# Two pairs in place of a group of four, second products at half the rate among pairs, x by DMA from tile 8 on, and a shorter lead for late tiles, in a fused retention and MLP kernel

## The chip, the cores and the metric

The kernel runs on one core of one Trainium2 chip. The metric is device time in microseconds (us), the median of several executions. The **span** is what the trace covers, from the first to the last instruction of the program; the time of an execution is some 1.8 to 2.1 us longer than its span. The engines are PE (matmuls), PEld (PE's weight loads, which overlap matmuls), DVE (VectorE), ACT (ScalarE), POOL (GpSimd) and SP (SyncE, which here only issues DMAs).

## The reference, cut to what matters

Retention over 768 steps with a decaying state, then one MLP block with a layer norm and a residual:

```python
for t in range(S):
    state = gamma[None, :, None, None] * state + np.einsum('bhd,bhe->bhde', k[:, :, t], v[:, :, t])
    y[:, :, t] = scale * np.einsum('bhd,bhde->bhe', q[:, :, t], state)
...
x = np.ascontiguousarray(attn_out.transpose(0, 2, 1, 3)).reshape(B, S, H * D)
xn = (x - mu) / np.sqrt(var + 1e-06) * g_ln
ch = np.maximum(xn @ w_ch1, 0.0) @ w_ch2
return x + ch
```

Batch 4, 8 heads, 64 values a head: 3072 rows of 512, and an MLP of 512 to 2048 to 512.

## The kernel before

The 3072 rows are 24 **tiles** of 128. For each tile the attention part makes, in this order, the scores `pa` (PE), masked scores `asb` (DVE), the output `py` (PE), its statistics and the normalised `xn` (DVE). Between chunks of a sequence, `pd` (PE) and `state` (DVE) carry the state; `vg` is v scaled on POOL for it. `trq` is q, transposed (from tile 8 on by a DMA from SP, into `tr`) and then scaled on DVE. Then x must stand transposed (`xnt`) for the **first product** (`mm`, 512 to 2048, in 16 blocks called `ho`), a ReLU on ACT, and the **second product** (`tp`, back to 512).

First products are made for groups of tiles, so that a matmul has 128, 256 or 512 columns:

```python
GROUPS = [1] * 6 + [2] * 3 + [4] * 3
...
T0, TX = 8, 11
```

x is transposed on PE for tiles below `TX`, by four matmuls against the identity and a copy by ACT. For tiles 8 to `TX` - 1 they write into the one buffer of the attention output, `py`, for earlier ones into a buffer of the second product, `tp`. From `TX` on x is transposed by a DMA from SP:

```python
if t < TX:
    xp = "tp" if t < T0 else "py"
    def e_tx(eng, t=t, xp=xp):
        p = take(xp, ("x", t), [P, KO, P], BF16)
        for ko in range(KO):
            nc.tensor.transpose(p[:, ko, :], held["xn", t][:, ko * P:(ko + 1) * P], idn)
    ...
else:
    def e_ex(eng, t=t, xb=xb, xi=xi):
        ...
        nc.sync.dma_start_transpose(out=held["xnt", xb][:, xi], in_=held["xn", t])
```

The order on every engine is made while the program is built. A small planner inside the kernel simulates the engines with assumed durations and picks, of the tasks that can start first, the one of lowest rank. Ranks come from a line of PE units, in which second products of earlier tiles (`behind`) are mixed among first products, and the attention of a tile comes 48 units ahead of its first product:

```python
for g in range(NG):
    for ho in range(HO):
        unit["1", g, ho] = u
        u += GROUPS[g] / 4
        if g >= 6 and ho % 4 == 3 and behind:
            unit["2", behind.pop(0)] = u
            u += 4
    behind += range(G0[g], G0[g] + GROUPS[g])
...
rank_of[t] = 10 * t if t < 4 else max(10 * t, 500 + unit["1", g, 0] - 48 + 8 * i)
```

So a changed rank moves instructions on all engines, and the engines then run what stands in their queues in that fixed order. The semaphores, not the planner, decide when.

Of the kernel before, what the change touches and what calls it, by code (L numbers as in the profile page):

```python
# [112 lines left out]
def kernel(  # L113
# [25 lines left out]
    HO = DH // P  # L139
    NPAIR = H // 2  # L140
    TILES = [(b, 0) for b in range(B)] + [(b, c) for b in range(B) for c in range(1, C)]
    number = {bc: t for t, bc in enumerate(TILES)}
    GROUPS = [1] * 6 + [2] * 3 + [4] * 3
    NG = len(GROUPS)
    G0 = [sum(GROUPS[:g]) for g in range(NG)]
    GMAX = max(GROUPS)
    T0, TX = 8, 11

    buf_of = {g: divmod(G0[g], GMAX) for g in range(NG)}
    group_of = {G0[g] + i: (g, i) for g in range(NG) for i in range(GROUPS[g])}  # L150

# [212 lines left out]
    unit, u, behind = {}, 0, []  # L364
    for g in range(NG):
        for ho in range(HO):
            unit["1", g, ho] = u
            u += GROUPS[g] / 4
            if g >= 6 and ho % 4 == 3 and behind:
                unit["2", behind.pop(0)] = u  # L370
                u += 4
        behind += range(G0[g], G0[g] + GROUPS[g])
    for t in behind:
# [3 lines left out]
    rank_of = {}  # L377
    for t in range(NT):
        g, i = group_of[t]
        rank_of[t] = 10 * t if t < 4 else max(10 * t, 500 + unit["1", g, 0] - 48 + 8 * i)  # L380


    ex, pbt, vgs, pbs = {}, {}, [], []
# [1 line left out]
    for t in range(NT):  # L385
        b, c = TILES[t]
        r = rank_of[t]
        g, i4 = group_of[t]
# [216 lines left out]
    for t, cols in [(t, slice(0, DM)) for t in range(NT - 1)] + [  # L605
            (NT - 1, slice(0, DM - P)), (NT - 1, slice(DM - P, DM))]:
        g, i4 = group_of[t]
# [70 lines left out]
```

## Time and profile before

| | before |
|---|---|
| time, first median of 3 | 217.09 us (216.86 to 217.13) |
| PE busy | 206.9 us, 96% of the profile's span |
| DVE, ACT, POOL busy | 56%, 40%, 42% |
| scaling of q from DMA'd tiles (`trq<-tr`), 16 times | 591 ns on average |

The profile is of another execution, of 217.65 us, 0.6 us over the median; its span is 215.8 us. What carries the reading stands in the prediction. Beside it, three groups of PE, with the counts that the change will move (busy us, mean ns | idle before):

```profile
L581 PE MATMUL mm<-xnt,w 128*128 128x512 bf16 x192 | 45.9, 379 | 0.0
...
L581 PE MATMUL mm<-xnt,w 128*128 128x256 bf16 x192 | 23.6, 273 | 0.0
...
L534 PE MATMUL py<-idn,xn 128*128 128x128 bf16 x12 | 1.2, 219 | 0.0
```

The mean of one matmul (379 ns) is not its price: matmuls overlap, and the price is the distance from one start to the next, 216 ns for 512 columns. One more group of the page, on DVE:

```profile
L425 DVE TENSOR_TENSOR trq<-tr,qsc 128x512 bf16<-128x512 bf16 x16 | 9.5, 591 | 0.3
```

### The profile page before, as it was taken

What the parts mean: (1) busy time and instruction counts of PE and PEld (TensorE: products, weight loads), DVE (VectorE), ACT (ScalarE), POOL (GpSimd) and SP (SyncE); (2) the same over time, 40 slices, a digit from 0 to 9 for tenths busy, and PEclk for the clock granted to TensorE, in tenths of its full rate; (3) what the DMA queues carried; (4) which work ended last, traced back from release to release, by engine and by line L of the source; (5) the groups of instructions that cost most, each with busy time, mean ns of one, the idle gap of its engine ahead of it and who ended that gap; (6) DMA issues with size and microseconds to landing.
All of it is one profiled execution on the core that took longest, in us unless ns stands there. A gap on an engine that the chain in (4) does not pass through costs nothing.

```text
span 215.8 us, 4578 instructions
## 1 busy us (share of the span) xinstructions
PE 206.9 (96%) x1892; PEld 130.7 (61%) x1910; DVE 120.3 (56%) x229; ACT 86.2 (40%) x158; POOL 89.7 (42%) x105
## 2 busy tenths in 40 slices
PE   7888899999999999999999999999999999999993
PEld 6777899996665567566757544554544444444442
DVE  6677577993029987999899955861511101111121
ACT  5466557774223235333316543563442334332000
POOL 8997699959953169863497100000000000000000
PEclk9999999999999999999999999999999999999999
DMA  7999999999999999999999993111121011110212
GB/s 140 179 180 181 178 155 196 206 163 150 165 162 206 153 203 146 164 143 183 184 153 177 110 225 98 49 24 29 47 73 49 3 49 49 49 49 0 100 49 97
DMA packets 106694, 26.51 MB, mean 123 GB/s; under 512 B 99377, under 2 KB 103729, under 8 KB 106674
## 3 DMA queue, kind: packets, MB, share of 16 engines
q0 software_dynamic: 75984, 13.24, 79.5%
q1 hardware_dynamic: 29506, 12.66, 31.3%
q10 hardware_dynamic: 1184, 0.33, 0.7%
q8 instruction: 15, 0.25, 0.5%
q14 instruction: 5, 0.04, 0.1%
HBM read 27.27 MB, written 6.29 MB: 155 GB/s over the span
## 4 chain that ended last, share of the span: by engine, by line
PE 86%; DMA 9%; POOL 1%; DVE 1%; issue 1%; POOLq 0%
PE tp L618 38%; PE mm L581 37%; DMA w<-in_moe_w_ch_dram 9%; PE pa L435 3%; PE pd L504 2%; PE py L458 2%; PE py L454 2%; DVE asb L442 1%; PE tp L534 1%; DVE trq L425 0%; POOL k L338 0%; PE tp L403 0%; PE tp L396 0%; POOL qsb L338 0%; POOL v L338 0%
## 5 line engine op out<-in xcount | busy, mean ns | idle before, releaser
L581 PE MATMUL mm<-xnt,w 128*128 128x128 bf16 (+2 forms) x768 | 94.3, 273 | 1.3 <-DMA w<-in_moe_w_ch_dram 0.9
L618 PE MATMUL tp<-w,h 128*128 128x512 bf16 (+2 forms) x382 | 86.4, 370 | 1.1 <-issue 0.2
L594 ACT ACTIVATE h<-mm 128x512 bf16<-128x512 f32 x92 | 55.0, 598 | 75.9 <-PE mm L581 75.6
L581 PEld LDWEIGHTS <-w 128*128 128x128 bf16 x768 | 58.4, 98 | 25.9 <-DMA w<-in_moe_w_ch_dram 1.3
L618 PEld LDWEIGHTS <-h 128*128 128x128 bf16 x400 | 37.4, 98 | 39.1
L626 DVE SCALAR_TENSOR_TENSOR osb<-tp,rstd,x_all 128x512 f32<-128x512 f32 (+2 forms) x25 | 18.2, 729 | 68.3 <-PE tp L618 68.2
L442 DVE TENSOR_TENSOR asb<-pa,mask 128x1024 bf16<-128x1024 f32 x24 | 29.3, 1219 | 7.2 <-PE pa L435 7.1
L472 DVE BATCH_NORM_STATS2 bns<-py 128x6 f32<-128x512 f32 x24 | 16.7, 697 | 10.4 <-PE py L458 10.1
L478 ACT CAST x_all<-py 128x512 bf16<-128x512 f32 x24 | 14.0, 584 | 17.1 <-DVE xn L467 15.7
L491 POOL TENSOR_TENSOR vg<-vsb,vsc 128x512 bf16<-128x512 bf16 x16 | 17.2, 1077 | 7.4 <-DMA vsb<-in_v_dram 3.6
L338 POOL DMA_DIRECT2D vsb<-in_v_dram x20 | 18.1, 908 | 2.6 <-PE py L458 2.6
L338 POOL DMA_DIRECT2D qk<-in_k_dram x16 | 14.7, 918 | 10.7 <-DMA tr<-qk 8.8
L467 DVE SCALAR_TENSOR_TENSOR xn<-py,mv,gb 128x512 bf16<-128x512 f32 x24 | 18.0, 751 | 1.2 <-DVE mv L473 0.3
L518 DVE TENSOR_TENSOR state<-pd,gch 64x256 bf16<-64x256 f32 x40 | 16.7, 418 | 0.8 <-PE pd L504 0.5
L338 POOL DMA_DIRECT2D qk<-in_q_dram x16 | 14.3, 892 | 3.2 <-DMA w<-in_moe_w_ch_dram 2.3
L425 DVE TENSOR_TENSOR trq<-tr,qsc 128x512 bf16<-128x512 bf16 x16 | 9.5, 591 | 0.3
L642 PE MATMUL mm<-zeros 128*128 128x128 bf16 x88 | 8.6, 260 | 1.0 <-DVE zeros L217 1.0
L458 PEld LDWEIGHTS <-asb 128*128 128x128 bf16 x192 | 7.8, 98 | 0.3 <-DVE asb L442 0.3
L458 PE MATMUL py<-vsb,asb 128*128 128x64 bf16 x160 | 7.9, 193 | 0.0
L642 PEld LDWEIGHTS <-zeros 128*128 128x128 bf16 x88 | 7.1, 119 | 1.2 <-DVE zeros L217 1.0
L454 PE MATMUL py<-state,trq 128*128 128x128 bf16 x80 | 7.7, 219 | 0.0
L454 PEld LDWEIGHTS <-trq 128*128 128x128 bf16 x80 | 5.8, 98 | 2.3
(65 smaller groups left out, 114.6 us busy)
## 6 DMA issues: line engine op xcount, KB each, us to landing
out_dram<-osb SPq DMA_DIRECT2D x23, 256.0 KB, 2.0
w<-in_moe_w_ch_dram POOLq DMA_DIRECT2D x8, 512.0 KB, 9.8
vsb<-in_v_dram POOLq DMA_DIRECT2D x20, 128.0 KB, 9.4
qk<-in_k_dram POOLq DMA_DIRECT2D x16, 128.0 KB, 8.2
qk<-in_q_dram POOLq DMA_DIRECT2D x16, 128.0 KB, 8.0
qsb<-in_q_dram POOLq DMA_DIRECT2D x7, 128.0 KB, 7.6
ksb<-in_k_dram POOLq DMA_DIRECT2D x4, 128.0 KB, 8.6
k<-in_k_dram POOLq DMA_DIRECT2D x3, 128.0 KB, 7.4
```

The costliest lines, as they stand in the source:

```text
L338: nc.gpsimd.dma_start(out=tile_of(kind, j), in_=src)
L442: nc.vector.tensor_tensor(out=take("asb", t, [P, NPAIR, 2, P], BF16).rearrange("p i a t -> p a i t"), in0=held["pa", t], in1=mask.rearrang ...
L454: nc.tensor.matmul(py[:, 2 * i:2 * i + 2, :], lhsT=held["trq", t][:, i, :], rhs=held["pb", t][:, i, :], start=(mi == 0), stop=False)
L458: nc.tensor.matmul(py[:, h, :], lhsT=held["asb", t][:, h // 2, h % 2, :], rhs=tile_of("v", t)[:, h, :], start=(mi == 0), stop=(mi == n - 1))
L467: nc.vector.scalar_tensor_tensor(out=take("xn", t, [P, DM], BF16), in0=held["py", t].rearrange("p h d -> p (h d)"), scalar=mv[:, t, 0:1], ...
L472: nc.vector.bn_stats(out=bns[:, t, :], in_=held["py", t].rearrange("p h d -> p (h d)"))
L491: e.tensor_tensor(out=take("vg", j, [P, H, D], BF16), in0=tile_of("v", j), in1=vsc[:, cc, :].unsqueeze(2).to_broadcast([P, H, D]), op=ALU. ...
L518: nc.vector.tensor_tensor(out=held["pb", n][o, :, o], in0=held["pd", b][o, :, o], in1=gch[o, cc, :].unsqueeze(2).to_broadcast([D, NPAIR, D ...
L581: nc.tensor.matmul(p[:, j, :], lhsT=w1[:, ko, (ho + j) * P:(ho + j + 1) * P], rhs=held["xnt", hb][:, h0:h0 + n, ko, :], start=(ko == 0), s ...
L594: nc.scalar.activation(out=dst, in_=src, func=AF.Relu)
L618: nc.tensor.matmul(held[key], lhsT=held["h1", hb][:, ho, i * P:(i + 1) * P], rhs=w2[:, ho, cols], start=(ho == 0), stop=(ho == HO - 1))
L626: nc.vector.scalar_tensor_tensor(out=take("osb", key, [P, w], FP32), in0=held[key], scalar=rstd[:, t:t + 1], in1=x_all[:, t, cols], op0=AL ...
```

## The change

Its intent: keep second products in stock as filler for PE while attention is made, give tiles 12 to 15 their first product earlier, and take three more transposes of x off PE.

```diff
-    GROUPS = [1] * 6 + [2] * 3 + [4] * 3
+    GROUPS = [1] * 6 + [2] * 5 + [4] * 2
...
-    T0, TX = 8, 11
+    T0, TX = 8, 8
...
-            if g >= 6 and ho % 4 == 3 and behind:
+            if g >= 6 and (ho + 1) % (HO // GROUPS[g]) == 0 and behind:
...
-        rank_of[t] = 10 * t if t < 4 else max(10 * t, 500 + unit["1", g, 0] - 48 + 8 * i)
+        rank_of[t] = 10 * t if t < 4 else max(10 * t, 500 + unit["1", g, 0] - (48 if t < 16 else 42) + 8 * i)
```

The third edit halves the **rate** of second products among pairs: one to every eight `ho` instead of one to every four. For groups of four it stays one to every four.

## The prediction

> **What bounds the kernel now.** I read the page's busy shares, its chain that ended last, the chain in order of time, the busy time by stretch, and last the waits of the matrix engine (PE). The page gives the first answer:
>
> ```profile
> PE 206.9 (96%) x1892; PEld 130.7 (61%) x1910; DVE 120.3 (56%) x229; ACT 86.2 (40%) x158; POOL 89.7 (42%) x105
> ...
> PE 86%; DMA 9%; POOL 1%; DVE 1%; issue 1%; POOLq 0%
> ```
>
> PE is busy for 96% of the span and makes 86% of the chain that ended last; the 9% of DMA are loads of the first weights, before 23.4 us. A busy PE need not be a PE at its peak, so next the chain in order of time (start, length, what), at tiles 10 and 18:
>
> ```profile
> 75.82 0.22 PE py L534 x4
> 76.04 1.73 PE tp L618 x8
> ...
> 113.85 1.85 PE mm L581 x16
> 115.70 0.22 PE pd L504 x4
> 115.92 0.87 PE mm L581 x8
> 116.80 0.22 PE py L454 x4
> 117.02 0.23 PE py L458 x8
> 117.25 1.73 PE mm L581 x8
> ```
>
> Each piece begins where the one before it ended. The lengths give the price of each piece: 4 transposes of x cost 0.22 us, 8 matmuls of 512 columns 1.73 us (0.216 each), 16 of 256 columns about 1.75 us (0.109 each; the 1.85 shown has the tail of a score product in it). Then the busy time by stretch (length, PE, PEld, DVE, ACT, POOL, clock, DMA):
>
> ```profile
> 57.00:75.00 18.00, 17.72 (x144) 10.44 (x145) 10.82 (x17) 4.23 (x8) 7.98 (x9) 1.00 1.81 180
> 75.00:95.00 20.00, 19.63 (x203) 13.93 (x205) 17.79 (x32) 7.90 (x15) 16.58 (x18) 1.00 1.74 172
> 95.00:115.00 20.00, 19.84 (x189) 12.71 (x190) 18.64 (x32) 5.57 (x11) 12.75 (x15) 1.00 1.74 163
> 115.00:126.00 11.00, 10.95 (x91) 6.31 (x90) 9.22 (x18) 6.00 (x11) 3.26 (x4) 1.00 1.85 161
> 126.00:160.00 34.00, 33.84 (x228) 16.55 (x230) 17.48 (x30) 15.56 (x27) 0.00 (x0) 1.00 0.29 71
> ```
>
> From 57 to 160 us PE is busy 101.98 of 103.00 us: all its idle time there is **1.0 us**, and part of that is matmul records missing from the trace. In the same stretch VectorE (DVE) runs at 89 to 93% from 75 to 115 us: it is the second engine to watch. The list of PE's waits agrees: no wait in this stretch is over 0.6 us, and the longest waits in it are the first weights' and the first tile's.
>
> **What the Trainium skill says.** (1) "TensorE: Matmul & The Clock Gate", section "Wait — 56ns, not 53.3ns?": matmuls back to back start N / 2.4 GHz plus about 2.5 ns apart. The trace agrees: 0.055, 0.109 and 0.216 us for 128, 256 and 512 columns, so halving the columns costs almost nothing. (2) The same page, "Step-by-step: what each phase is for": the next weights load while this matmul runs. The trace agrees: a weight load takes 98 ns, less than the 109 ns of a matmul of 256 columns. (3) "DMA: Bandwidth & Descriptors", section "Issuing engines are not separate DMA queues": all DMAs share 16 engines. Here the transposes from SyncE take a median 6.4 us from issue to landing, 7 to 9 us while loads run and 2.4 us after 130 us. (4) "SBUF — State Buffer", section "Who interferes with whom": a DVE operation with two SBUF inputs can be blocked by a GpSimd operation that reads SBUF. Here the scaling of q takes 0.42 us alone and up to 1.2 us where it meets GpSimd's scaling of v.
>
> **The change part by part.** How the order moves I took from the two programs' instruction orders; up to about 57 us (the state product of tile 9) they are the same on every engine.
>
> Removed from PE: the transposes of x of tiles 8, 9 and 10, three times 0.22 = **-0.67 us**. ScalarE loses three copies of 0.59 us, which did not bound anything.
>
> Added to PE: the first product of tiles 12 to 15 was 64 matmuls of 512 columns, 64 x 0.216 = 13.84 us; it becomes 128 of 256 columns, 128 x 0.1094 = 14.00 us: **+0.16 us**. The 64 extra weight loads (6.3 us of PEld) lie beside matmuls. The second products keep their number and size. So PE's work changes by **-0.51 us**.
>
> Added elsewhere: three transposes by DMA, each 1.2 us of SyncE's queue and some 6 us to land; one more square root (0.3 us of ScalarE) and reciprocal (0.17 us of DVE).
>
> Moved: second products run at half the rate among the pairs, so six instead of four are left for the end. That end is pure PE work in both kernels and PE's total decides, so this gives and takes nothing. The first product of tiles 8 and 9 moves from before the attention product of tile 12 to after that of tile 11, those of tiles 12 to 15 move forward by some 8 us and more, and the attention of tiles 20 to 23 comes 1.4 to 4 us earlier on PE.
>
> The idle 1.0 us could shrink or grow. I summed PE's work and DVE's work between one tile's output product and the next, in the new order. PE, tiles 13 to 17: three first-product pieces of 0.87, one second-product quarter of 0.86 (or a fourth piece), 0.33 + 0.22 + 0.45 of attention = **4.47 us** a tile. DVE from one start to the next: mask 1.13, state 0.88, scaling 0.45, statistics 0.95, x 0.66 = **4.1 us**, 4.2 with a reciprocal and 4.7 with an output addition. So PE is slightly the slower of the two in most tiles, and DVE in those with an addition (tiles 10 to 11, 13 to 14), where it has about 1 us in hand. I expect about as much idle time as before, at most a little more: +0.2. Chosen sum: 217.09 - 0.51 + 0.2 - 0.2 (py's buffer no longer held by the transposes) = 216.6; I put it at **216.5 us**.
>
> **The rivals.** (a) *DVE becomes the bound* from tile 12 to 20, because the second products that filled PE between attention pieces are fewer. For it: DVE's 93%, and scalings that stretch to 1.2 us, which would take 0.7 us of the 1 us in hand. Against it: before, tiles 16 to 19 already ran at 4.6 us a tile with PE full. If eight tiles each lose 0.3 us: +2.4, about 218.5. (b) *Landing of transposed q and k becomes the wait.* The load of tile 20 waits for a buffer that the transpose of tile 18 frees; before, its own transpose landed at 120.8 us and DVE took it at 121.6, so 0.8 us were left. Now PE wants tile 20's scores some 2 us earlier, and three more transposes share the queue. Likewise x of tile 19, which lands after the transpose of tile 23 is issued (126.8 before): the new order needs it at about 132, where before it had until about 141. Worth 0 to 3 us: up to 219.5. (c) *x of tiles 8 to 10 late.* Against it: 13 us lie between x of tile 11 and its product, and landing takes at most 9.3. Worth nothing. (d) *All idle time goes*: 217.09 - 0.51 - 1.0 = 215.6, the floor.
>
> **Range and chances.** The floor gives the low end with a little for run noise (0.3 us between runs), 215.3; (a) or (b) at half their size gives the high end, 218.6. Faster by 2% needs 4.3 us, which PE's work and idle time do not hold: 1%. Slower by 2% needs (a) and (b) in full together: 3%.
>
> **What would show each step.** PE's matmuls among the first products of 256 columns go from 192 to 320, those of 512 from 192 to 128, the x transposes into py vanish. PE busy from 57 to 160 us stays above 101 of 103 us if I am right on idle time; under (a) PE waits on DVE's masked scores or on scaled q between 85 and 125 us; under (b) DVE shows gaps ahead of the scaling of q with the DMA into tr as their cause, or PE waits for xnt near 131 us. The prediction is wrong if such waits sum to over 2 us, or if the time falls below 215.3, which would mean idle time that I did not see.

## The result, and the profile after

The changed kernel took **216.0 us** (median of 4, 215.78 to 216.07) against 217.06 for the kernel before in the same rounds. The ratio is 0.9951, 95% interval 0.9934 to 0.9968. Ratios here are the mean time of one kernel's fast runs over that of the other's of the same rounds, so not quite the ratio of the medians quoted. A second timing, of the control among the experiments below, gave 215.78 against 216.88, ratio 0.9949. So the change is worth 1.1 us, half a per cent, clear of noise and far below 2%.

The page of the changed kernel:

```profile
PE 206.9 (97%) x1962; PEld 135.8 (63%) x1962; DVE 118.6 (55%) x230; ACT 84.2 (39%) x156; POOL 89.5 (42%) x105
...
PE 87%; POOL 5%; DMA 5%; DVE 1%; ACT 1%; issue 0%; POOLq 0%
```

PE is still nearly the whole chain; the bound has not moved. Its groups show the intended counts, and the transposes into `py` are gone:

```profile
L581 PE MATMUL mm<-xnt,w 128*128 128x256 bf16 x320 | 39.3, 273 | 0.0
L581 PE MATMUL mm<-xnt,w 128*128 128x512 bf16 x128 | 30.4, 379 | 0.0
```

The busy time by stretch (length, PE, PEld, DVE, ACT, POOL, clock, DMA), for the same stretches as in the prediction:

```profile
57.00:75.00 18.00, 18.00 (x135) 10.07 (x133) 10.80 (x18) 3.86 (x7) 8.69 (x10) 1.00 1.80 179
75.00:95.00 20.00, 20.00 (x207) 13.73 (x206) 17.80 (x32) 6.68 (x13) 14.96 (x17) 1.00 1.77 197
95.00:115.00 20.00, 20.00 (x226) 15.84 (x225) 17.80 (x33) 10.62 (x21) 12.25 (x14) 1.00 1.86 154
115.00:126.00 11.00, 11.00 (x124) 8.83 (x122) 8.69 (x17) 6.08 (x11) 4.43 (x5) 1.00 1.72 147
126.00:160.00 34.00, 34.00 (x231) 17.25 (x230) 16.11 (x28) 12.53 (x23) 0.00 (x0) 1.00 0.31 70
```

PE is busy for 103.00 of 103.00 us. **Three warnings belong to this.** First, the idle time of the kernel before in this view (1.0 us) is partly an artefact. Its trace lacks some matmul records: the page counts 382 matmuls of the second product where the changed kernel's counts all 400, and each missing one leaves a gap of about 0.05 us (0.432 us between two starts, less 0.379 us of modelled duration). I therefore measured idle time again from start to start of PE's matmuls, setting aside gaps as long as exactly one missing matmul. That gives 0.6 us of real waiting for the kernel before and none for this profile. Second, this profile was a lucky execution: the control's profile shows 0.4 us of waiting. Third, the two spans differ by 1.8 us, and not all of it is the change: the kernel before reaches the state product of tile 9, up to which both orders are the same, at 56.94 us, the changed one at 56.48.

The chain in order of time, at tiles 17 and 18:

```profile
108.11 0.33 PE pa L435 x8
108.44 0.98 PE mm L581 x8
109.42 0.22 PE pd L504 x4
109.64 0.87 PE mm L581 x8
110.52 0.22 PE py L454 x4
110.74 0.23 PE py L458 x8
```

From one output product to the next it is now all first product and attention, 4.6 us from tile 16 to 17 (105.91 to 110.52), piece against piece. The prediction's 4.47 us lacked the 0.11 us that the piece after each `pa` takes longer (0.98 against 0.87).

DVE's group of scaled q became cheaper, though it does the same work:

```profile
L425 DVE TENSOR_TENSOR trq<-tr,qsc 128x512 bf16<-128x512 bf16 x16 | 7.7, 480 | 1.7 <-DMA tr<-qk 1.4
```

Its mean fell from 591 to 480 ns, which is 1.8 us of DVE. The cause of the long ones, and what they do to PE, is the subject below. The idle 1.4 us at its end is DVE waiting for the transposed q and k of tile 20 to land, at 121.6 us.

### The profile page after: what moved, and what is told of

Read it like the earlier page. It is cut to its first block, busy times and chain, and to the rows that moved or that the text cites. A ratio compares the mean times of both kernels' runs of the same rounds, so it can differ in the third digit from the quotient of the medians.

```text
span 214.0 us, 4707 instructions
## 1 busy us (share of the span) xinstructions
PE 206.9 (97%) x1962; PEld 135.8 (63%) x1962; DVE 118.6 (55%) x230; ACT 84.2 (39%) x156; POOL 89.5 (42%) x105
## 4 chain that ended last, share of the span: by engine, by line
PE 87%; POOL 5%; DMA 5%; DVE 1%; ACT 1%; issue 0%; POOLq 0%
PE tp L618 39%; PE mm L581 38%; DMA w<-in_moe_w_ch_dram 5%; PE pa L435 3%; PE py L458 2%; PE pd L504 2%; PE py L454 2%; POOL qsb L338 1%; POOL k L338 1%; POOL v L338 1%; POOL vg L491 1%; PE tp L396 0%; PE tp L534 0%; POOL ksb L338 0%; POOL vsb L338 0%; PE tp L403 0%
## 5 line engine op out<-in xcount | busy, mean ns | idle before, releaser
L618 PE MATMUL tp<-w,h 128*128 128x512 bf16 (+2 forms) x400 | 89.3, 371 | 0.0
L581 PEld LDWEIGHTS <-w 128*128 128x128 bf16 x832 | 64.5, 98 | 20.9 <-DMA w<-in_moe_w_ch_dram 0.5
L425 DVE TENSOR_TENSOR trq<-tr,qsc 128x512 bf16<-128x512 bf16 x16 | 7.7, 480 | 1.7 <-DMA tr<-qk 1.4
```

The costliest lines, as they stand in the source:

```text
L581: nc.tensor.matmul(p[:, j, :], lhsT=w1[:, ko, (ho + j) * P:(ho + j + 1) * P], rhs=held["xnt", hb][:, h0:h0 + n, ko, :], start=(ko == 0), s ...
L618: nc.tensor.matmul(held[key], lhsT=held["h1", hb][:, ho, i * P:(i + 1) * P], rhs=w2[:, ho, cols], start=(ho == 0), stop=(ho == HO - 1))
```

## The experiments

**The theory:** time is PE's work plus PE's waits; the change cuts the work by 0.5 us and, by its order, the waits by another 0.5 to 0.6 us. **The rivals:** the gain is the pairs' alone, and work taken off PE comes back as waiting; the held `py` buffer makes the waits; the lead makes the order free of waits; PE has hidden slack, so its work does not count fully.

Twelve kernels ran, each beside the kernel before on the same chip, with 5 rounds each. All gave the right result. "Work" is the change of PE's work against the kernel before, from the prices in the prediction. "Rest" is the change of the median span less that work: what the order did, and, for the kernels with `TX` of 8 or less, a quarter of a us at the end of the program, of which more below the table.

| kernel | time, us | ratio to before (95%) | span | PE work | rest |
|---|---|---|---|---|---|
| before | 216.88 to 216.98 | | 215.1 to 215.2 | | |
| after_again | 215.78 | 0.9949 (0.9937 to 0.996) | 214.0 | -0.5 | -0.6 |
| lead_undone | 215.8 | 0.9951 (0.9939 to 0.9963) | 214.0 | -0.5 | -0.6 |
| x_alone | 216.65 | 0.9985 (0.9972 to 0.9998) | 214.6 | -0.7 | +0.2 |
| pairs_alone | 216.97 | 1.0005 (0.9993 to 1.0016) | 214.9 | +0.2 | -0.4 |
| x_undone | 216.69 | 0.9988 (0.9977 to 1.0) | 214.75 | +0.2 | -0.6 |
| rate_alone | 216.88 | 1.0002 (0.9989 to 1.0015) | 214.8 | 0 | -0.3 |
| rate_undone | 217.0 | 1.0001 (0.9985 to 1.0017) | 215.05 | -0.5 | +0.4 |
| x_other_buffer | 217.27 | 1.002 (1.0008 to 1.0032) | 215.3 | 0 | +0.1 |
| pe_extra | 219.4 | 1.0128 (1.0106 to 1.0149) | 217.6 | +3.1 | -0.6 |
| pe_extra_before | 220.55 | 1.0159 (1.0145 to 1.0173) | 218.75 | +3.6 | +0.1 |
| x_from_7 | 217.5 | 1.0025 (0.9998 to 1.0052) | 215.7 | -0.7 | +1.3 |
| x_from_6 | 220.36 | 1.016 (1.0131 to 1.019) | 218.6 | -1.0 | +4.4 |

Read the last column from above: every kernel with the halved rate, and x by DMA from no tile before 8, has a rest of -0.3 to -0.6 us. Every kernel with the old rate has one of +0.1 to +0.4 us. Spans carry this reading; a part of the time outside the span (1.8 us for before, after_again, lead_undone, the two with extra work, x_from_6 and x_from_7, and 1.9 to 2.1 us for the six others) differs from kernel to kernel, and no run shows why. It is the reason that x_alone, pairs_alone and rate_alone look worse by time than by span.

**A part of the gain is not of the order at all.** The profiles show it after PE's last matmul. From that matmul's start to the end of the span are 3.57 to 3.61 us in the six kernels with `TX` = 11, 3.32 to 3.37 us in the seven with 8 or 7, and 3.22 us in x_from_6. At its end the program lets SP check the semaphores of its DMAs in a fixed order, 0.06 us each. After the last output has landed there are seven checks to go with `TX` = 11, four with 8, three with 7 and two with 6. The lines of SP's semaphore instructions at the end, of the kernel before and of the changed one:

```profile
L673 SPq EVENT_SEMAPHORE  x10: 17/28/28, 214.2 to 215.8; - x10
L673 SPq EVENT_SEMAPHORE  x7: 17/28/28, 212.6 to 213.9; - x7
```

The three checks are 0.18 us, and the last output also lands some 0.05 us sooner (1.65 against 1.70 us after the last addition). So about 0.25 us of the gain comes with the three DMAs of x. As I read it from these counts, they shift the place of the last output in that list. Without it the rest is -0.35 us for the changed kernel, -0.3 to -0.6 us for all with the halved rate and `TX` of 8 or 11, and +0.1 to +0.6 us for all with the old rate.

**What is left of the rest is waits of PE.** I compare the time from the state product of tile 9 to PE's last matmul, less the work of the table. In after, pairs_alone, x_undone, rate_alone and pe_extra, all with the halved rate, it is 154.7 us, the same within 0.02 us, and no start-to-start distance of PE's matmuls shows a wait. In after_again and lead_undone it is 0.4 us more. With the old rate it is 0.5 us more in pe_extra_before, 0.6 in the kernel before and in x_other_buffer, 0.7 in rate_undone and 0.85 in x_alone. These are single executions.

### Does PE's work count one to one? pe_extra and pe_extra_before

Four useless matmuls ahead of the scores of tiles 8 to 23, overwritten by the scores. The order of everything else is the same.

```diff
             pa = take("pa", t, [P, 2, NPAIR, P], FP32)
+            if t >= T0:
+                for _ in range(4):
+                    nc.tensor.matmul(pa[:, 0, 0, :], lhsT=zeros, rhs=zeros, start=True, stop=True)
             for i in range(NPAIR):
```

On the changed kernel (pe_extra):

> The changed kernel in the same order with 4 useless matmuls of 128 columns (0.22 us) ahead of the scores of each of the 16 tiles from 8 on, overwritten by the scores: 3.6 us more PE work. Theory (PE is full and nothing hides work on it): 219.5 to 219.7. Rival (DVE or DMA is nearly the bound beside it, and part of PE's time in 57 to 160 us is slack that the trace hides): under 218.5.

Measured: 219.4 us, 3.6 us over the 215.8 us of lead_undone, which is as fast as the changed kernel (215.78 in the control). That is the full price of the added work; the theory's range began 0.1 us higher, since it started from 216.0. On the kernel before (pe_extra_before):

> The kernel before with the same 4 useless matmuls ahead of the scores of tiles 8 to 23, 3.6 us more PE work in the same order. Theory (its 0.7 us of idle time is PE ahead of DVE by a little, so more work on PE swallows most of it): 219.8 to 220.3. Rival (the idle time stays, since each wait has its own cause): 220.5 to 220.7.

Measured: 220.55 us, 3.67 us over 216.88. (The 0.7 us of idle time named there is the 0.6 us of above, counted a little high.) My theory for this one fell, and the rival holds: added work swallows none of the waits. So work on PE counts one to one in both kernels, and the waits of the kernel before are not a general lag of DVE, but have their own causes at their own places. It follows that the 0.51 us of work less is worth 0.5 us.

### The parts: x_alone, pairs_alone, rate_alone

x_alone is the kernel before with `T0, TX = 8, 8`:

```diff
-    T0, TX = 8, 11
+    T0, TX = 8, 8
```

> The kernel before with x of tiles 8 to 10 transposed by DMA, nothing else. Theory (time = PE work + PE idle, and PE has no other slack): PE work falls by 3 x 0.22 = 0.67 us, so 216.1 to 216.6, depending on what the new order does to the 1.0 us of idle time. Rival (the work taken off PE is given back as waiting, and the gain of the changed kernel comes from its pairs alone): 216.9 to 217.2, with PE idle from 57 to 160 us grown by about 0.7 us.

Measured: 216.65 us, 0.3 us gained (one execution of five, 220.32 us, was slow and is left out of the ratio). That lies 0.05 us above the theory's range, and 0.25 us below the rival's. The span fell by 0.5 us, where the work and the end of the program together would give 0.9: some 0.4 us came back as waits. The trace names 0.6 us of waiting for scaled q; the view of the kernel before names 0.2.

```profile
PE pa L435 <- DVE trq L425: 0.6, 2, 0.3
```

pairs_alone is the kernel before with the new groups and the new rate:

```diff
-    GROUPS = [1] * 6 + [2] * 3 + [4] * 3
+    GROUPS = [1] * 6 + [2] * 5 + [4] * 2
-            if g >= 6 and ho % 4 == 3 and behind:
+            if g >= 6 and (ho + 1) % (HO // GROUPS[g]) == 0 and behind:
```

> The kernel before with the new groups (tiles 12 to 15 as two pairs) and the new rate of second products, x of tiles 8 to 10 still through PE, lead 48. Theory: PE work grows by 0.16 us; the new order takes away the idle time, up to 0.6 us of the 1.0: 216.6 to 217.2. Rival (the pairs bring the whole gain): 216.0. Rival (x through PE holds the one py buffer, so the idle time stays): 217.2 to 217.5.

Measured: 216.97 us, nothing gained by time, 0.2 us by span. The rival that gave the pairs the whole gain is out. rate_alone has the new rate with the old groups:

```diff
-            if g >= 6 and ho % 4 == 3 and behind:
+            if g >= 6 and (ho + 1) % (HO // GROUPS[g]) == 0 and behind:
```

> The kernel before with the new rate of second products among its three pairs, groups of four kept for tiles 12 to 23, x of tiles 8 to 10 through PE. PE's work is that of before. Theory A (the rate, by keeping second products as filler for the attention of the pairs, is what takes the idle time): 216.3 to 216.7. Theory B (rate and pairs need each other, since groups of four want their attention early): 216.9 to 217.5.

Measured: 216.88 us, the same by time, 0.3 us less by span. By time that is theory B. By span it is theory A in part, and in its profile PE waits nowhere after 57 us, as theory A says. What hides this in the time is the time outside the span, 2.1 us here against 1.8 us for the kernel before, whose cause is open.

### Leave one out: lead_undone, x_undone, rate_undone

lead_undone is the changed kernel with the lead of 48 for all tiles:

```diff
-        ... 500 + unit["1", g, 0] - (48 if t < 16 else 42) + 8 * i)
+        ... 500 + unit["1", g, 0] - 48 + 8 * i)
```

> The changed kernel with the lead of 48 units for all tiles. Theory: PE's work is the same to the instruction, and PE was full from 57 us on, so the lead matters only if PE waits without it: 216.0 to 216.4. Rival (the lead is what makes the new order free of waits): 216.5 or more, with PE waiting on tr, trq or asb of tiles 16 to 23.

Measured: 215.8 us, as fast as the changed kernel. The shorter lead gives nothing.

x_undone is the changed kernel with `T0, TX = 8, 11`:

```diff
-    T0, TX = 8, 8
+    T0, TX = 8, 11
```

> The changed kernel with x of tiles 8 to 10 through PE again, lead 42 and pairs kept. Theory (work plus idle): 0.67 us more work than the changed kernel and at most 0.4 us of idle time from the held py buffer: 216.5 to 217.1. Rival (the gain of the change was the pairs, and x alone is worth 0.3 us as it was on the kernel before): 216.1 to 216.4.

Measured: 216.69 us, 0.9 us more than the changed kernel, within the theory's range. By span it is 0.75 us: the 0.67 us of work and 0.25 us of the program's end, less about 0.2 us of waits, for this profile shows no wait, with the `py` buffer held as before. So with the rest of the change in place x by DMA is worth its work and a little more by time, not the 0.3 us that it was worth alone.

rate_undone is the changed kernel with the old rate:

```diff
-            if g >= 6 and (ho + 1) % (HO // GROUPS[g]) == 0 and behind:
+            if g >= 6 and ho % 4 == 3 and behind:
```

> The changed kernel with second products among the pairs at the old rate, one to every four ho. PE's work is the same to the instruction. Theory: the rate only orders the work, PE stays nearly full: 216.0 to 216.5. Rival (the rate is what keeps DVE ahead: with twice the second products among pairs the attention of tiles 16 to 23 comes later and bunches up): 216.6 or more, with PE waiting on trq or asb of late tiles.

Measured: 217.0 us (216.5 to 217.42). **The whole gain is gone**, with PE's work the same to the instruction; the rival holds. In its trace PE waits twice for scaled q (0.6 us in all), as in x_alone.

### The buffer: x_other_buffer

The kernel before, x of tiles 8 to 10 still through PE but into the two buffers of the second product:

```diff
-            xp = "tp" if t < T0 else "py"
+            xp = "tp"
```

> The kernel before, x of tiles 8 to 10 still through PE, but written to the buffers of the second product (tp, two of them) in place of the one buffer of the attention output (py). PE's work is the same. Theory: if the held py buffer was the cause of PE's idle time after tile 8 the time falls by up to 0.5 us (216.4 to 216.8); rival (those waits come from DVE, the buffer costs nothing): 216.8 to 217.2.

Measured: 217.27 us, slightly slower. The held `py` buffer does not cost what I thought, or its relief costs as much again in the new order. Either way, no gain from it is seen. The waits in its profile, 0.6 us, have nothing to do with scalings of q: PE waits before a state product at 70.98 us and for x of a tile at 73.28 us.

### The control: after_again

The changed kernel, unaltered.

> The changed kernel unaltered, as a control beside the runs below, on one chip with them. Theory: 215.8 to 216.1, and PE without idle time from 57 to 160 us again, as in its first profile. If PE shows 0.3 us or more of waits this time, the idle time differs from one execution to the next and single profiles are not to be read to a tenth of a us.

Measured: 215.78 us. Its profile is not free of waits, though; the second outcome came true. The view of PE's waits has this:

```profile
PE pa L435 <- DVE trq L425: 0.4, 1, 0.4
```

and in order of time on POOL, DVE and PE (start, length, what, idle before and its releaser):

```profile
82.28 1.08 POOL L491 TENSOR_TENSOR vg<-vsb,vsc 128x512 bf16<-128x512 bf16 x1
82.31 1.34 DVE L425 TENSOR_TENSOR trq<-tr,qsc 128x512 bf16<-128x512 bf16 x1
...
83.80 0.40 PE L435 MATMUL pa<-trq,tr 64*128 64x128 bf16 x8 [0.37 <-DVE trq L425]
```

POOL's scaling of v runs from 82.28 to 83.36; DVE's scaling of q, which takes 0.42 us alone, begins 0.03 us later and ends at 83.65; PE stands before the scores until 83.80. The first profile of the same kernel had at this place a scaling of 0.43 us, at 82.49, and no wait: in the two executions the same instructions met, or missed each other, by tenths of a us. **Most of PE's waits are made of such collisions with POOL.** Of 16 scalings in each of the fourteen profiles (224), 55 took over 0.5 us, and all 55 overlap work of POOL: 50 a scaling of v (two of them only in their last 0.02 us, after 1 us beside DMA issues), and 5 DMA issues alone. The 115 that met no work of POOL took 0.41 to 0.43 us. Every wait of PE for `trq` of these tiles, in the control, x_alone, lead_undone, rate_undone and the kernel before, follows a long one.

The kernel before shows the same at tile 9, beside a scaling of v:

```profile
66.47 1.04 POOL L491 TENSOR_TENSOR vg<-vsb,vsc 128x512 bf16<-128x512 bf16 x1 [2.25 <-DMA vsb<-in_v_dram]
...
66.64 1.15 DVE L425 TENSOR_TENSOR trq<-tr,qsc 128x512 bf16<-128x512 bf16 x1
...
67.93 0.40 PE L435 MATMUL pa<-trq,tr 64*128 64x128 bf16 x8 [0.18 <-DVE trq L425]
```

and at tile 17, by a group of loads that POOL issues:

```profile
107.61 1.20 DVE L425 TENSOR_TENSOR trq<-tr,qsc 128x512 bf16<-128x512 bf16 x1
...
107.90 0.90 POOL L338 DMA_DIRECT2D qk<-in_k_dram  x1
...
108.87 0.40 PE L435 MATMUL pa<-trq,tr 64*128 64x128 bf16 x8
```

The scaling ends at 108.81 and the scores begin 0.06 us after it: PE began them at once, and nothing stood between. From start to start the wait is 0.07 us here, 0.17 us at tile 14 (beside DMA issues too) and 0.24 us at tile 9: 0.5 of the 0.6 us that this profile waits. The other 0.1 us is before a state product, at 97.80 us. In the first profile of the changed kernel that distance is 2.2 us at tile 17, and 0.2 us or more at every tile.

### More of the same: x_from_6 and x_from_7

If PE is full, taking x of tiles 7 and 6 off it too should give 0.22 us each. x_from_6 is the changed kernel with `TX = 6`:

```diff
-    T0, TX = 8, 8
+    T0, TX = 8, 6
```

> The changed kernel with x by DMA from tile 6 on: two more tiles, 2 x 0.22 = 0.45 us less PE work. Theory (PE is full, work converts one to one): 215.4 to 215.7 if the new order has no waits. Rival (x of tile 7 lands too late, 7 to 9 us after its issue with loads in flight, and PE waits for it near 62 us): 216.0 or more, with a wait of PE for xnt.

Measured: 220.36 us, 4.6 us slower than the changed kernel. The rival holds, though at another tile than I named: PE waits 4.1 us for x of tile 11.

```profile
PE mm L581 <- DMA xnt<-xn: 4.1, 1, 4.1
```

The chain shows its way: the DMA was issued at 90.73 us, behind an output store in SP's queue, and took 9.5 us to land, while the planner's new order wanted it at 96. The wait costs more than itself. The busy time by stretch, around it (after the stretch and its length come PE, PEld, DVE, ACT and POOL, then the granted clock and two figures of DMA):

```profile
96.00:100.30 4.30, 0.24 (x4) 0.01 (x1) 2.09 (x4) 0.97 (x2) 3.93 (x5) 0.96 2.05 123
100.30:103.40 3.10, 3.10 (x23) 2.44 (x24) 0.33 (x1) 0.60 (x1) 0.06 (x1) 0.50 1.52 204
103.40:110.00 6.60, 6.55 (x77) 5.11 (x77) 5.70 (x12) 3.51 (x7) 1.86 (x2) 1.00 1.97 162
```

After 4.06 us of idling PE's granted clock is 0.50 for 3.1 us, so about 1.5 us more are lost. The Trainium skill tells of this in "TensorE: Matmul & The Clock Gate", section "HAM oscillation — how this bites in real kernels": no PE idle gaps of more than about 3.4 us. This trace agrees.

x_from_7, with `TX = 7`, was meant as a kernel faster than both:

```diff
-    T0, TX = 8, 8
+    T0, TX = 8, 7
```

> The changed kernel with x by DMA from tile 7 on, one tile more: 0.22 us less PE work. Theory (PE full, work converts, and here the first product of tiles 6 and 7 comes 14 us of PE work after x of tile 7): 215.6 to 215.8. Rival (a DMA of x queued behind an output store lands too late, as with x from tile 6 on): 216.5 or more, with a wait of PE for xnt.

Measured: 217.5 us, with executions from 216.47 to 218.57. Both guesses missed: x landed in time, but in its profile the scaling of q for tile 8 took 2.06 us, first beside a DMA issue and then beside a scaling of v, and PE waited 1.1 us for it. Why its other executions spread over 2 us is open. So no kernel beats the changed one; lead_undone equals it.

## Why the prediction was right or wrong

**The range, the class and the bound: right.** 216.0 us lies in 215.3 to 218.6, the change is within 2%, and PE stayed the bound. The point, 216.5, was 0.5 us too high (0.7 by the control).

**The work term, -0.51 us: right, and shown.** The counts are as predicted (320 and 128 matmuls, no transposes into `py`), and both runs with extra matmuls show that PE's work counts one to one: 3.6 us added, 3.6 and 3.67 us measured.

**The idle term: wrong in sign; this is the step that failed.** The prediction expected "about as much idle time as before, at most a little more: +0.2". Instead, of the measured 1.1 us, 0.51 us is work, about 0.25 us the program's end, of which the prediction knew nothing, and about 0.35 us waits of PE that the order took away. The outcome is near the prediction's rival (d), "All idle time goes", which I had treated as the floor. My sums of PE's and DVE's work per tile had the right sizes, but a sum over a tile cannot show the waits. They sit where scores follow closely upon a scaling of q that meets POOL. I had the collision in hand, 0.42 against up to 1.2 us, and counted it against the change instead of asking how often each order meets it. I also put the 1.2 us down to the scaling of v; that scaling (tile 17) met DMA issues alone.

**"Second products run at half the rate ... this gives and takes nothing": wrong.** rate_undone has the same PE work and loses the whole gain, 1.2 us by time against lead_undone, 1.05 us by span. I looked at the end, where the six stored second products do no harm, and not at the middle, where the order of all engines changes with them. That the halved rate removes waits is shown, by rate_undone and by the rests and profiles above. Through what exactly, which scaling is moved away from which POOL work, is read from single profiles, and those differ from execution to execution; so the detailed path is argued, not shown.

**The held buffer, -0.2 us: not supported.** x_other_buffer took that hold away and gained nothing, and x_undone has the hold and no wait in its profile.

**Rival (a), DVE as the bound: did not happen.** PE had no lasting wait for DVE in either profile of the changed kernel, with 4.6 us of PE from tile 16 to 17, measured, against 4.1 to 4.7 us of DVE, computed from the durations before.

**Rival (b), late transposes of q and k: half right.** DVE waited 1.4 us for tile 20's at 121.6 us, the place and time that I named. PE lost nothing by it: it began tile 20's scores at 123.67 us. Nor did it wait for x of tile 19.

**Rival (c), x of tiles 8 to 10 late: right that it is worth nothing here.** x_from_6 shows the limit: with another order the same kind of DMA cost over 4 us.

**"Wrong ... if the time falls below 215.3": did not occur.** That the floor held is partly luck: the idle time of 1.0 us from which I took it was 0.4 us too high, since part of it was missing records, and the 0.25 us of the program's end was missing from it. With both put right the floor is 217.1 - 0.5 - 0.6 - 0.25, about 215.7, and the kernel came out at 215.8 to 216.0 with 0 and 0.4 us of waits in its two profiles.

**Slips in the sums.** For rival (a) 2.4 us on top of the point of 216.5 is 218.9, not 218.5, and half of (a) or (b) on top of it ends at 218.0, so the high end of 218.6 does not follow from the working. The median of 6.4 us from issue to landing is that of x alone; the transposes of q and k in the same queue took 7.7 us. None of these decided the outcome.

**The lead of 42:** the prediction gave it no term of its own, and lead_undone shows that it needs none.

## What to carry to other kernels

When one engine fills the span, its work is the sure part of an estimate, one to one; the order of the rest decides a remainder that can be as large, and two edits that each seem idle can be worth more together than apart. Look for waits not in averages per tile but at the places where the full engine follows closely upon an operation whose length varies, and give it something to do there. Before crediting an order with what is left of a gain, look at what comes after the full engine's last instruction. Before moving work to a DMA, find what stands ahead of it in its queue and how long it takes to land while loads run.

## What the Trainium skill lacked or had wrong

- "SBUF — State Buffer", section "Who interferes with whom": a DVE operation with two SBUF inputs contends with a GpSimd operation that reads SBUF. The runs agree, and add the length: in 47 cases the long DVE scaling ends 0.28 to 0.30 us after POOL's does (82.31 + 1.34 against 82.28 + 1.08 in the control), for 0.42 us of work of its own.
- The same section infers that such an operation and descriptor generation for DMAs need different interfaces of the ports that DVE and GpSimd share, so that they don't meet. In 37 of the 42 cases in which a scaling met DMA issues alone that fits (0.41 to 0.43 us), but in five it took 0.55, 0.57, 0.72, 1.01 and 1.20 us, the last shown above, and two more took 1.01 and 1.14 us with a scaling of v only in their last 0.02 us. What sets them apart is open.
- No page prices the change between matmuls of 64 and of 128 rows; "TensorEngine Tiling (Array Packing)", section "Key Properties", has only that a change of tiling mode drains the engine. Here the piece after each group of scores, which are the matmuls of 64 rows, takes 0.98 us in place of 0.87 us. That the change of rows is the cause is not shown.
- No page tells of time outside the span that depends on the kernel: 1.8 us for the changed kernel and up to 2.1 us for pairs_alone, and 1.8 us for lead_undone beside that 2.1.
- No page tells of the checks at the program's end: 0.06 us for each DMA semaphore on SP, with seven or four of them after the last landing, 0.25 us between two kernels whose PE does the same there.
